# Reordering the first batch of a linear-attention and SwiGLU kernel: k's exp and maximum earlier, the second q.z between two k.v terms

## The chip, the cores and the metric

One core of one Trainium2 chip. The metric is device time in microseconds (us) of the whole kernel, one number per run, compared as medians. Ratios are the mean time of one kernel's fast runs over the mean of the other's fast runs of the same rounds, so they are not quite the ratio of the medians quoted beside them. Times within a profile are us from the span's start. In its lines PE is TensorE, PEld TensorE's loading of weights, DVE VectorE, ACT ScalarE and POOL GpSimd; L292 is line 292 of the kernel. The granted clock is the share of its full clock that TensorE was given; each run comes with its mean.

## The reference

```python
def phi(x):                                   # elu(x) + 1
    return np.where(x > 0, x, np.exp(x) - 1.0) + 1.0
q_p, k_p = phi(q), phi(k)                     # batch 8, heads 8, seq 576, dim 64
kv  = einsum('bhsd,bhse->bhde', k_p, v)
z   = sum(k_p, axis=2)
x   = (q_p @ kv) / (q_p . z + 1e-6)           # 4608 x 512 after a transpose
out = (silu(x @ w_gate) * (x @ w_val)) @ w_out   # 512 -> 1536 -> 512
```

The kernel computes phi as max(x, 0) + min(exp(x), 1). For k these are two tensors, `kp` (the maximum) and `ek` (exp, then the minimum with 1); their sum is phi(k). A product with phi(k) can be taken as one term of the sum, or as two terms that TensorE accumulates.

## The kernel before

The long middle of the kernel is layer 1 and layer 2 of the feed-forward block (`l1`, the matmuls of L292, and `l2`, L299). Before it stands a prologue for batch 0, scheduled by hand. In its profile each engine's instructions come in the order of these calls: k's first half landed at 7.43, but its maximum, which stands behind three q products on VectorE, ran at 8.56.

```python
    # helpers, cut to their effect (lp: first or second half of the heads)
    # exp_k(b,lp)  ScalarE  ek = exp(k)              mx_k  VectorE  kp = max(k, 0)
    # mn_k         VectorE  ek = min(ek, 1)          add_k VectorE  kp = ek + kp
    # q_exp/q_phi  ScalarE / VectorE: the same for q, transposed, four pieces
    # zt(.., kp|ek)        TensorE  sum over the sequence (z), term by term
    # zr_copy              VectorE  Zr <- PSUM
    # t_corners(g, Zr|R)   TensorE  q.z or q.kv, four 64x64 corners
    # lnrd                 ScalarE  rd = exp(-ln(q.z)), two pieces of 512 columns
    # kv_corner(.., kp|ek) TensorE  k.v, 36 small matmuls;  r_copy VectorE  R <- PSUM
    # x_t                  VectorE  xT = q.kv * rd (one PSUM bank each)
    # l1_mm(g, f, ps, c)   TensorE  chunk c of layer 1 (L276)
    # warm(n)              TensorE  n idle matmuls on ones
    ...
    q_exp(1, 0, qb)
    q_exp(1, 1, qb)
    exp_k(0, 0)
    warm(WARM[2])
    exp_k(0, 1)
    q_phi(0, 0, qa); q_phi(0, 1, qa); q_phi(1, 0, qb)
    mx_k(0, 0)
    q_phi(1, 1, qb)
    mn_k(0, 0)
    mx_k(0, 1)
    zt(0, 0, X[1], kp, True, False)
    warm(WARM[3])
    zt(0, 0, X[1], ek, False, True)
    zr_copy(0, 0, X[1])
    warm(WARM[4])
    t_corners(0, Zr, 0, pp4[2])
    lnrd(pp4[2], 0)
    add_k(0, 0)
    mn_k(0, 1)
    zt(0, 1, Y[0], kp, True, False)
    kv_corner(0, 0, kp, True, True)
    r_copy(0, 0, 1, "VV")
    zt(0, 1, Y[0], ek, False, True)
    warm(WARM[5], ps=X[0])
    zr_copy(0, 1, Y[0])
    t_corners(0, R, 0, X)
    x_t(0, 0, X, (0,))
    kv_corner(0, 1, kp, True, False)
    kv_corner(0, 1, ek, False, True)
    r_copy(0, 1, 2, "VV")
    t_corners(0, Zr, 1, Y)
    lnrd(Y, 1)
    x_t(0, 0, X, (1,))
    l1_mm(0, 0, pp4[2], (0,))
    l1_mm(0, 1, X, (0,))        # its second bank is the one that x_t(.., (1,)) reads
    t_corners(0, R, 1, pp4[1])
    x_t(0, 1, pp4[1])
    for c in (1, 2, 3):
        l1_mm(0, 0, pp4[2], (c,)); l1_mm(0, 1, X, (c,))
    ...
```

## Time and profile before

| | before |
|---|---|
| median of the first runs | 313.73 us (313.45 to 314.19) |
| span of the profiled run | 311.8 us |
| TensorE busy | 98% of the span |
| TensorE's share of the chain that ended last | 95% |
| first matmul of L292, layer 1 at full width | 18.18 us |
| third q exp on ScalarE (a reference point used below) | 7.23 us |

In the profile a matmul of L292 lasts 0.38 us and the next one starts 0.22 us after it: the records overlap, so TensorE's busy share is not what to aim at. What the reader needs is where TensorE waits, and after 18.18 us it practically doesn't. The prediction below shows the chain and VectorE's timeline. ScalarE's timeline of the kernel before (columns: start, length, engine, line, operation, written and read tile, shape, count).

```profile
6.41 2.09 ACT L120 ACTIVATE qT<-pp,m 128x512 f16<-128x512 f32 x3
8.39 2.21 ACT L120 ACTIVATE ek<-kr 128x1152 f16<-128x1152 f16 x2
```

k's two exps start at 8.39, right behind q's last piece, and no idle time is noted before them: they wait for ScalarE, not for the load of k, which landed at 7.43.

### The profile page before, as it was taken

The numbers are of one execution on the slowest core, as the hardware profiler recorded it, in microseconds if no ns is written. First come the engines' busy times: TensorE is split into PE (matmuls) and PEld (weight loads), VectorE is DVE, ScalarE is ACT, GpSimd is POOL, SyncE is SP. The second block draws the span as 40 slices with busy tenths as digits, with TensorE's granted clock in tenths as the row PEclk, the third lists the DMA queues.
The fourth block names the chain that finished last, engine by engine and source line by source line (L and its number), as shares of the span: only waits on it lengthen the run. The fifth ranks groups of instructions, "written<-read, shape, count | busy, mean of one in ns | idle before, by whom it ended". The sixth has DMA issues, their size and how long they took to land.

```text
span 311.8 us, 5565 instructions
## 1 busy us (share of the span) xinstructions
PE 305.4 (98%) x2206; PEld 142.0 (46%) x2206; DVE 205.1 (66%) x361; ACT 152.7 (49%) x231; POOL 48.7 (16%) x73
## 2 busy tenths in 40 slices
PE   7999999999999999999999999999999999999994
PEld 3444454444544454445444544454444444444442
DVE  4855878999599658976697759874981434143410
ACT  4865959538733844374536643574330333033311
POOL 8745444400000410041000500000000000000000
PEclk9999999999999999999999999999999999999998
DMA  8999999999502593239512990323032300240014
GB/s 216 196 198 200 206 206 236 235 206 148 116 15 39 98 196 109 40 58 189 156 38 41 132 233 13 63 52 87 0 75 60 78 1 1 45 92 0 2 34 101
DMA packets 41178, 32.80 MB, mean 105 GB/s; under 512 B 16448, under 2 KB 36160, under 8 KB 41152
## 3 DMA queue, kind: packets, MB, share of 16 engines
q0 software_dynamic: 20480, 18.29, 37.4%
q1 hardware_dynamic: 20592, 14.13, 19.1%
q8 instruction: 17, 0.28, 0.3%
q14 instruction: 9, 0.07, 0.1%
q10 hardware_dynamic: 80, 0.03, 0.0%
HBM read 37.75 MB, written 9.44 MB: 151 GB/s over the span
## 4 chain that ended last, share of the span: by engine, by line
PE 95%; DVE 2%; DMA 1%; SPq 0%; issue 0%; ACT 0%; DVEq 0%
PE pp L292 58%; PE pp L299 30%; PE pp L276 2%; PE pp L254 2%; PE pp L185 2%; DMA q<-in_q_dram 1%; DVE qT L454 1%; PE pp L124 1%; DVE xT L425 0%; PE pp L412 0%; PE pp L212 0%; PE pp L374 0%; DVE osb L322 0%; SPq L333 0%; DVE qp L467 0%
## 5 line engine op out<-in xcount | busy, mean ns | idle before, releaser
L120 ACT ACTIVATE sil<-pp 128x512 f16<-128x512 f32 x108 | 63.4, 597 | 100.8 <-PE pp L292 98.4
L292 PE MATMUL pp<-xT,wg 128*128 128x512 f16 x416 | 106.8, 379 | 0.0
L292 PE MATMUL pp<-xT,wv 128*128 128x512 f16 x416 | 106.8, 379 | 0.0
L285 DVE SCALAR_TENSOR_TENSOR hT<-pp,sil 128x512 f16<-128x512 f32 x108 | 72.3, 681 | 48.0 <-PE pp L292 35.3
L299 PE MATMUL pp<-wo,hT 128*128 128x512 f16 (+2 forms) x444 | 97.1, 373 | 0.6 <-DVE osb L322 0.6
L299 PEld LDWEIGHTS <-hT 128*128 128x128 f16 x444 | 41.9, 98 | 49.9 <-issue 2.1
L292 PEld LDWEIGHTS <-wv 128*128 128x128 f16 x416 | 40.7, 98 | 49.1
L292 PEld LDWEIGHTS <-wg 128*128 128x128 f16 x416 | 40.7, 98 | 48.5
L322 DVE TENSOR_SCALAR osb<-pp 128x512 f32<-128x512 f32 (+1 forms) x19 | 12.9, 681 | 31.1 <-PE pp L299 26.7
L120 ACT ACTIVATE osb<-pp 128x512 f32<-128x512 f32 (+1 forms) x18 | 10.3, 574 | 34.8 <-PE pp L299 34.8
L120 ACT ACT_TABLE_LOAD x13 | 16.7, 1283 | 2.5 <-PE pp L292 2.4
L120 ACT ACTIVATE ek<-kr 128x1152 f16<-128x1152 f16 x16 | 17.8, 1157 | 0.1
L710 POOL COPY gate<-qT 128x1 f16<-128x1 f16 x4 | 1.5, 374 | 95.9 <-DMA qT<-qp 95.9
L229 DVE TENSOR_TENSOR qp<-qp,rden 128x1152 f16<-128x1152 f16 x12 | 16.2, 1347 | 0.0
L220 DVE TENSOR_REDUCE den<-prod 128x18 f32<-128x1152 f16 x12 | 16.1, 1342 | 0.0
L120 ACT ACTIVATE eq<-qr 128x1152 f16<-128x1152 f16 x14 | 15.6, 1151 | 0.1
L271 DVE TENSOR_SCALAR xT<-pp 128x512 f16<-128x512 f32 (+1 forms) x14 | 8.8, 667 | 6.8 <-PE pp L254 6.8
L103 POOL DMA_DIRECT2D vr<-in_v_dram x16 | 11.8, 740 | 8.8 <-DMA wo<-in_moe_w_out_dram 2.4
L103 POOL DMA_DIRECT2D kr<-in_k_dram x16 | 11.5, 722 | 7.9 <-DMA wo<-in_moe_w_out_dram 1.9
L159 DVE TENSOR_TENSOR kp<-ek,kp 128x1152 f16<-128x1152 f16 x15 | 11.4, 758 | 0.5
L147 DVE TENSOR_SCALAR ek<-ek 128x1152 f16<-128x1152 f16 x16 | 8.0, 500 | 5.0 <-ACT ek L120 5.0
L103 POOL DMA_DIRECT2D qr<-in_q_dram x14 | 10.1, 724 | 5.6 <-DMA qr<-in_q_dram 2.6
(86 smaller groups left out, 180.0 us busy)
## 6 DMA issues: line engine op xcount, KB each, us to landing
out_dram<-osb SPq DMA_DIRECT2D x70, 128.0 KB, 2.8
kr<-in_k_dram POOLq DMA_DIRECT2D x16, 288.0 KB, 8.7
vr<-in_v_dram POOLq DMA_DIRECT2D x16, 288.0 KB, 9.7
qr<-in_q_dram POOLq DMA_DIRECT2D x14, 288.0 KB, 11.6
wg<-in_moe_w_gate_dram POOLq DMA_DIRECT2D x5, 256.0 KB, 9.5
wv<-in_moe_w_val_dram POOLq DMA_DIRECT2D x5, 256.0 KB, 10.1
q<-in_q_dram SPq DMA_DIRECT2D x2, 576.0 KB, 4.2
wo<-in_moe_w_out_dram POOLq DMA_DIRECT2D x2, 512.0 KB, 12.4
```

The lines of the kernel that those rows point to most:

```text
L103: nc.gpsimd.dma_start(out=dst[b % NB][:, 2 * lp:2 * lp + 2, :], in_=src[b].rearrange("(l a) (c j) d -> (a c) l (j d)", a=2, j=J)[:, 2 * lp ...
L120: nc.scalar.activation(out=out, in_=in_, func=func, bias=bias, scale=scale)
L147: nc.vector.tensor_scalar(out=a, in0=a, scalar1=1.0, scalar2=None, op0=ALU.min)
L159: nc.vector.tensor_tensor(out=a, in0=ek[b % 2][:, lp, :, :], in1=a, op=ALU.add)
L185: nc.tensor.matmul(out=ps[hh][D * l2:D * l2 + D, D * lp:D * lp + D], lhsT=t[b % 2][rows, lp, j, D * l2:D * l2 + D], rhs=vr[b % NB][rows, 2 ...
L220: nc.vector.tensor_reduce(out=den[:, c, :], in_=prod[:, :, :].rearrange("p j (l d) -> p (j l) d", d=D), axis=AX.X, op=ALU.add)
L229: nc.vector.tensor_tensor(out=qv, in0=qv, in1=rden[:, c, :].unsqueeze(2).to_broadcast([P, 2 * J, D]), op=ALU.mult)
L271: nc.vector.tensor_scalar(out=dst, in0=ps[l2][:, c0:], scalar1=1.0 / SC, scalar2=None, op0=ALU.mult)
L285: nc.vector.scalar_tensor_tensor(out=hT[g % 2][:, fb, :], in0=ps[1][:, :], scalar=SC, in1=s[:, :], op0=ALU.mult, op1=ALU.mult)
L292: nc.tensor.matmul(out=ps[h][:, :], lhsT=w[:, c, P * fb:P * fb + P], rhs=xT[g % 2][:, c, :], start=(c == 0), stop=(c == 3))
L299: nc.tensor.matmul(out=l2p[(g, t)][:, n0:n1], lhsT=hT[g % 2][:, fb, P * t:P * t + P], rhs=wo[:, fb, n0:n1], start=(fb == 0), stop=(fb == F ...
L322: nc.vector.tensor_scalar(out=o[:, n0:n1], in0=ps[:, n0:n1], scalar1=1.0 / SC, scalar2=None, op0=ALU.mult)
```

## The change

The intent: start k's first half earlier on ScalarE and VectorE, so that the first z and the first k.v come earlier; take the second half's maximum and minimum out of the way of the first sum; give the second q.z, and with it ScalarE's logarithms, a place ahead of the last k.v term.

```diff
-    WARM = (4, 2, 5, 4, 2, 1)
+    WARM = (4, 2, 5, 2, 2, 1)
     q_exp(1, 0, qb)
+    exp_k(0, 0)
     q_exp(1, 1, qb)
-    exp_k(0, 0)
     ...
+    mx_k(0, 0)
     q_phi(1, 0, qb)
-    mx_k(0, 0)
+    mn_k(0, 0)
     q_phi(1, 1, qb)
-    mn_k(0, 0)
-    mx_k(0, 1)
     ...
     add_k(0, 0)
-    mn_k(0, 1)
-    zt(0, 1, Y[0], kp, True, False)
+    mx_k(0, 1)
     kv_corner(0, 0, kp, True, True)
     r_copy(0, 0, 1, "VV")
-    zt(0, 1, Y[0], ek, False, True)
+    zt(0, 1, Y[0], kp, True, False)
     warm(WARM[5], ps=X[0])
-    zr_copy(0, 1, Y[0])
+    mn_k(0, 1)
     t_corners(0, R, 0, X)
     x_t(0, 0, X, (0,))
+    zt(0, 1, Y[0], ek, False, True)
+    zr_copy(0, 1, Y[0])
     kv_corner(0, 1, kp, True, False)
+    t_corners(0, Zr, 1, Y)
+    lnrd(Y, 1)
     kv_corner(0, 1, ek, False, True)
     r_copy(0, 1, 2, "VV")
-    t_corners(0, Zr, 1, Y)
-    lnrd(Y, 1)
     x_t(0, 0, X, (1,))
```

## The prediction

> **What bounds the kernel now.** I read the page's shares first, then the chain of waits, then the timeline of the first 19 us, because the change touches only the prologue of batch 0.
>
> ```profile
> PE 305.4 (98%) x2206; PEld 142.0 (46%) x2206; DVE 205.1 (66%) x361; ACT 152.7 (49%) x231; POOL 48.7 (16%) x73
> PE 95%; DVE 2%; DMA 1%; SPq 0%; issue 0%; ACT 0%; DVEq 0%
> ```
>
> TensorE carries 95% of the chain that ended last. Listing TensorE's idle gaps from 18.2 us to 306.9 us gives one of 0.03 us and no other over 0.02: once layer 1 runs at full width (L292, from 18.18 us), nothing but TensorE sets the pace. So the change is worth exactly what it does to the start of the first L292 matmul, now 18.18 us. It has no second place to act.
>
> The chain in order of time shows who sets that start:
>
> ```profile
> 8.64 0.38 DVE kp L143
> 9.02 0.05 issue
> 9.07 0.39 PE pp L412 x9
> ...
> 11.11 0.34 PE pp L254 x4
> ...
> 13.19 0.69 DVE xT L425
> 13.88 0.26 DVE R L201 x2
> 14.14 0.66 DVE xT L425
> 14.80 0.04 issue
> 14.85 0.38 PE pp L276
> 15.22 0.34 PE pp L254 x4
> 15.56 2.78 PE pp L276 x12
> 18.34 17.27 PE pp L292 x80
> ```
>
> The chain alternates between VectorE and TensorE until 14.80. The tail is what matters: the second xT product (14.10 to 14.79) frees a PSUM bank; the fourth L276 matmul, which writes that bank, starts at 14.85; behind it on TensorE stand the four last q.kv corners (15.15), then twelve L276 matmuls, then L292. The timeline names the same work:
>
> ```profile
> 9.58 0.62 DVE L147 TENSOR_SCALAR ek<-ek 128x1152 f16<-128x1152 f16 x1
> 10.69 0.29 DVE L416 TENSOR_SCALAR Zr<-pp 128x128 f16<-128x128 f32 x1
> 12.54 0.29 DVE L416 TENSOR_SCALAR Zr<-pp 128x128 f16<-128x128 f32 x1
> 13.19 0.69 DVE L425 SCALAR_TENSOR_TENSOR xT<-pp,rd 128x512 f16<-128x512 f32 x1 [0.36 <-PE pp L254]
> 13.79 0.35 DVE L201 CAST R<-pp 128x64 f16<-128x64 f32 x2
> 14.10 0.69 DVE L425 SCALAR_TENSOR_TENSOR xT<-pp,rd 128x512 f16<-128x512 f32 x1
> 15.67 0.69 DVE L425 SCALAR_TENSOR_TENSOR xT<-pp,rd 128x512 f16<-128x512 f32 x1 [0.87 <-PE pp L254]
> 16.58 0.69 DVE L425 SCALAR_TENSOR_TENSOR xT<-pp,rd 128x512 f16<-128x512 f32 x1 [0.22 <-ACT rd L120]
> ```
>
> Two chains end nearly together. The third product (15.67) releases chunk 2 of layer 1 at 16.41; the fourth waits for ScalarE's last reciprocal (ends 16.54) and releases chunk 3 at 17.32. Both must move for a gain; either alone can cause a loss.
>
> [...] k's first half landed at 7.43 us, yet its maximum (L143) ran only at 8.56, behind the third q product. [...] Here 512-column matmuls start 0.42 us apart at 1.06 us and 0.22 apart from 9.32 on; no idle gap is over 0.6 us[...]. [...] the minimum of ek took 0.62 us at 9.58, inside a GpSimd DMA issue (9.21 to 9.95), and 0.45 at 11.56, in a pause of it; that is 0.17 more, not a wait to the issue's end.
>
> **The change, part by part.** All durations are from this trace. "Pitch" is start to start where nothing waits: a q exp 0.59, a k exp 1.05, a 128x512 product on VectorE 0.61, a Zr copy 0.21, two R copies 0.30 to the next operation.
>
> *Front half: k's exp, maximum and minimum earlier.* The third q exp starts at 7.23; k's first exp follows at 7.82 (was 8.39) and ends at 8.98. The fourth q exp goes from 7.82 to 8.87, ending 9.55; the second k exp stays at 9.44. On VectorE, k's maximum starts at 7.26 + 0.61 = 7.87, the third q product at 8.23, k's minimum at 8.98 + 0.03 = 9.01 instead of 9.58. The fourth q product waits for its exp: 9.55 + 0.03 = 9.58. The Zr copy stands behind it, 9.58 + 0.61 = 10.19, against 10.69 now. Gain 0.50; the hoped-for 0.57 is clipped by the late q exp. Two warm-up matmuls (0.43 us) go out between the two k sums, which needs them gone: the second sum can now start near 9.5.
>
> *Middle.* Moving the second half's maximum and minimum behind the sum changes little on the path, since the sum started right after the Zr copy before as well: 10.19 + 0.21 = 10.40, ending 11.15. First k.v at 11.20 (was 11.70), R copies at 11.20 + 0.53 = 11.73, ready 12.09, R corners at 12.17 (was 12.67), first xT product at 12.17 + 0.52 = 12.69 (was 13.19). Still 0.50 ahead.
>
> *Tail: the new order of the second half.* Here the gain is spent. The second Zr copy was at 12.54, before the first product; now the minimum precedes and the second z sum follows the R corners, so the copy stands behind the first product: 12.69 + 0.61 = 13.30, ready 13.59. [...] the second q.z corners start at 13.59 + 0.06 = 13.65 (were at 13.50), and the second term of the last k.v, placed after them, at 13.65 + 0.24 = 13.89 (was 13.20). The R copies wait for that term, 0.53 after its start as in the first k.v: 14.42 (were 13.79, held there only by the first product). The second xT product is behind the R copies: 14.42 + 0.31 = 14.73, against 14.10. That is +0.63 on the chain shown. From there everything repeats: fourth L276 matmul 15.48 (14.85), last corners 15.79 (15.15), third product 16.30 (15.67), chunk 2 at 17.05 (16.41), then eight matmuls of 0.215: L292 at 18.77, against 18.18.
>
> *ScalarE's side.* Its second group of logarithms starts 0.45 after the corners, 14.10 against 13.98, so its last reciprocal ends at about 16.66 instead of 16.54. The fourth product would then run at 16.91, before chunk 3 needs it at 17.91. This chain no longer decides.
>
> Sum: −0.50 at the first product, +1.09 between first and second product (2.04 from start to start, was 0.91, less rounding), −0.05 where chunk 3 no longer waits: about **+0.6 us**. 313.73 + 0.59 = **314.3 us**. None of the removed or moved work was itself 2% of anything: 2% is 6.3 us, a third of the prologue.
>
> **The rivals.**
> 1. *The front gain survives.* If the author's intent holds, that is, if the second q.z corners start early and ScalarE's chain is the true bound, everything shifts by 0.4 to 0.5: 313.3. For it: the chain of waits runs through the first Zr copy, which does move. Against it: VectorE's order puts the R copies ahead of the second product in the changed kernel too, and they now wait for a k.v term that itself waits for the second Zr copy. This round trip was absent before.
> 2. *Only ScalarE's delay counts.* If I have the R copies too late, the logarithms' later start gives +0.1: 313.85.
> 3. *The clock relapses.* Two warm-up matmuls fewer, and new TensorE gaps of 0.3 us near 9.3 and 0.65 near 14.8. [...] Against it: before, TensorE already idled 0.56 us at 9.07, and was busy again.
> 4. *A load becomes the bound.* k's exp and maximum now want k at 7.8; it landed at 7.43, 0.4 to spare. The loads of v (10.40, 11.79) are needed at 11.20 and 12.8. A load later by 0.5 would undo the front gain, which adds at most 0.3 to the end.
>
> **Range and chances.** The three unprofiled times of before span 0.74 us, so a median may be off by 0.3; my steps of 0.02 to 0.06 add up to perhaps 0.25. That gives 313.8 to 314.8; for rivals 1, 2 and 3 I widen it to 313.6 to 315.0. Two per cent in either direction is out of reach of the stretch touched: faster 0.005, slower 0.01, the rest within.
>
> **What would show it.** Right: first Zr copy near 10.2; first xT product near 12.7; second Zr copy after it, near 13.3; the two last R copies near 14.4 with a wait for k.v (L185) before them; second xT product near 14.7; the fourth L276 matmul with about 0.65 us of TensorE idle before it; first L292 near 18.8. Wrong: R copies that start at 13.8 or sooner, or a first L292 before 18.2; matmuls of L276 0.43 apart would mean the clock; an exp of k with a wait for its load would mean rival 4.

Passages that no trace or run of this case bears out are cut from it, and the cuts are marked. The sum is −0.50, +1.09 and −0.05, put as about +0.6 us, and the forecast 313.73 + 0.59 = 314.3 us. That fewer warm-up matmuls and new gaps might lower the clock was the author's guess: the trace of the kernel before has a granted clock of 1.00 from 6.8 to 306.9 us. The tail's step from the q.z corners to the second k.v term took for granted that TensorE keeps the order of its calls; the changed kernel's trace shows that order (under "Why the prediction was right or wrong").

## The result

Changed 314.48 us (median of 4 runs, 314.39 to 314.52), before 313.59 us (4 runs, 313.40 to 314.19). The ratio is 1.0025, 95% interval 1.0007 to 1.0042: slower by a quarter of a per cent, which is "same" by the 2% measure. Both profiled runs are at a mean granted clock of 0.997.

The page of the changed kernel: busy shares, then the chain's shares by engine.

```profile
PE 305.6 (98%) x2204; PEld 141.9 (45%) x2204; DVE 204.5 (65%) x361; ACT 152.7 (49%) x231; POOL 48.6 (16%) x73
PE 95%; DVE 2%; DMA 2%; ACT 1%; issue 0%; SPq 0%; DVEq 0%
```

Nothing here tells the two kernels apart: four TensorE instructions fewer (two warm-up matmuls and their weight loads), the same shares. The chain in order of time does (start, length, what):

```profile
8.22 1.06 ACT ek L120
9.28 0.59 ACT qT L120
9.86 0.02 issue
9.89 0.69 DVE qT L454
10.58 0.20 DVE Zr L416
10.78 0.68 DVE kp L159
...
12.98 0.69 DVE xT L425
13.67 0.21 DVE Zr L416
13.88 0.04 issue
13.92 0.41 PE pp L254 x4
14.33 0.41 PE pp L185 x36
14.74 0.35 DVE R L201 x2
15.09 0.61 DVE xT L425
15.70 0.04 issue
15.74 0.38 PE pp L276
```

The chain runs from the first xT product (12.98) to the second Zr copy, the q.z corners, the k.v term, the R copies and the second product (15.09), where the chain of before went straight from the first product to the R copies and the second product. VectorE's timeline of the changed kernel shows the same and what it waited for (in brackets: idle time, and who ended it):

```profile
10.50 0.28 DVE L416 TENSOR_SCALAR Zr<-pp 128x128 f16<-128x128 f32 x1
12.98 0.69 DVE L425 SCALAR_TENSOR_TENSOR xT<-pp,rd 128x512 f16<-128x512 f32 x1 [0.23 <-PE pp L254]
13.59 0.28 DVE L416 TENSOR_SCALAR Zr<-pp 128x128 f16<-128x128 f32 x1
14.73 0.36 DVE L201 CAST R<-pp 128x64 f16<-128x64 f32 x2 [0.86 <-PE pp L185]
15.00 0.68 DVE L425 SCALAR_TENSOR_TENSOR xT<-pp,rd 128x512 f16<-128x512 f32 x1
```

VectorE stands idle for 0.86 us before the R copies, for k.v (L185). The first full L292 matmul starts at 19.03, 0.85 after that of before, and after it TensorE has one gap over 0.02 us up to the last batch, as before. The prologue's loss arrives whole at the end: in all 14 profiles of this document, 293.5 to 293.7 us pass from the first L292 matmul to the end of the span.

Part of the 0.85 has nothing to do with the order. The third q exp, which the change does not touch, started at 7.53 in this profile instead of 7.23, because q's second half landed at 6.07 instead of 5.90 and its cast then took 0.62 us instead of 0.43. So I compare the kernels by the **distance** from the third q exp to the first L292 matmul: 10.95 before, 11.50 changed, +0.55. The prediction's own times give 18.77 − 7.23 = 11.54.

### The profile page after: what moved, and what is told of

Read it like the earlier page. It is cut to its first block, busy times and chain, and to the rows that moved or that the text cites. A ratio compares the mean times of both kernels' runs of the same rounds, so it can differ in the third digit from the quotient of the medians.

```text
span 312.6 us, 5561 instructions
## 1 busy us (share of the span) xinstructions
PE 305.6 (98%) x2204; PEld 141.9 (45%) x2204; DVE 204.5 (65%) x361; ACT 152.7 (49%) x231; POOL 48.6 (16%) x73
## 4 chain that ended last, share of the span: by engine, by line
PE 95%; DVE 2%; DMA 2%; ACT 1%; issue 0%; SPq 0%; DVEq 0%
PE pp L292 57%; PE pp L299 30%; PE pp L276 2%; PE pp L254 2%; PE pp L185 2%; DMA q<-in_q_dram 2%; DVE xT L425 0%; ACT qT L120 0%; ACT ek L120 0%; DVE qT L454 0%; DVE kp L159 0%; PE pp L212 0%; DVE qp L467 0%; PE pp L374 0%; DVE osb L322 0%
## 5 line engine op out<-in xcount | busy, mean ns | idle before, releaser
L292 PE MATMUL pp<-xT,wg 128*128 128x512 f16 x416 | 106.8, 379 | 0.0
L292 PE MATMUL pp<-xT,wv 128*128 128x512 f16 x416 | 106.8, 379 | 0.0
L292 PEld LDWEIGHTS <-wv 128*128 128x128 f16 x416 | 40.7, 98 | 49.1
L292 PEld LDWEIGHTS <-wg 128*128 128x128 f16 x416 | 40.7, 98 | 48.4
```

The lines of the kernel that those rows point to most:

```text
L292: nc.tensor.matmul(out=ps[h][:, :], lhsT=w[:, c, P * fb:P * fb + P], rhs=xT[g % 2][:, c, :], start=(c == 0), stop=(c == 3))
```

## The experiments

Each was run in 5 rounds beside the kernel before and gave the reference's result. "k exp" is the start of the first k exp, "k lands" the landing of the half that it reads.

| run | median us | before beside it | ratio (95% interval) | distance | k lands | k exp |
|---|---|---|---|---|---|---|
| again | 314.34 | 313.53 | 1.0025 (1.0012 to 1.0037) | 11.72 | 8.00 | 8.03 |
| front_old_tail | 313.27 | 313.53 | 0.9989 (0.9975 to 1.0002) | 11.22 | 8.35 | 8.37 |
| new_tail_only | 314.51 | 313.53 | 1.0030 (1.0018 to 1.0043) | 11.91 | 7.35 | 8.35 |
| qz_behind | 313.91 | 313.53 | 1.0011 (0.9999 to 1.0024) | 11.11 | 7.48 | 8.16 |
| warm_four | 314.19 | 313.46 | 1.0023 (1.0011 to 1.0035) | 12.01 | 8.30 | 8.32 |
| x_before_r | 314.02 | 313.46 | 1.0027 (1.0010 to 1.0043) | 11.32 | 7.64 | 7.81 |
| before_k_swapped | 314.51 | 313.46 | 1.0032 (1.0016 to 1.0049) | 11.60 | 9.20 | 9.22 |
| changed_k_swapped | 316.27 | 313.46 | 1.0083 (1.0059 to 1.0107) | 14.04 | 8.89 | 8.91 |
| front_again | 313.84 | 313.55 | 1.0017 (0.9994 to 1.0041) | 10.51 | 7.25 | 7.81 |
| front_k_first | 313.34 | 313.55 | 0.9992 (0.9979 to 1.0004) | 10.51 | 7.43 | 7.98 |
| x_warm_four | 313.73 | 313.55 | 1.0005 (0.9993 to 1.0017) | 11.05 | 7.20 | 7.82 |
| front_k_first_warm | 313.61 | 313.69 | 0.9999 (0.9985 to 1.0012) | 10.70 | 7.68 | 7.98 |

Distance, landing and exp are of one profiled run each; the medians are of five or six runs, of which the profiled one need not be typical. The record numbers four different chips for the four sets of rounds, so absolute times are compared only within a set, as in the column "before beside it".

### The changed kernel again

No edit.

> The changed kernel once more, for a closer ratio and a second profile. In the one profile so far the third q exp started at 7.53 us, against 7.23 before, because q's second half landed later; from there to the first full layer 1 matmul (L292) it took 11.50 us, against 10.95 before. Theory A (the order of the tail costs it): that distance is a property of the order and comes back at 11.50 within 0.1, whatever the start of the third q exp, and the kernel is 0.5 to 0.7 us over the one before (ratio 1.0016 to 1.0022). Theory B (the later landing was part of the cost, for a reason in the change): the third q exp starts near 7.5 again and the kernel is 0.8 to 0.9 us over.

The third q exp was back at 7.22 and the kernel still 0.81 us over: theory B fell. But the distance was 11.72, not 11.50, so theory A was not the whole either. The difference, 0.22, is just what the first k exp lost: it started 0.81 after the third q exp instead of 0.59, because k's load landed at 8.00. A theory F came from this: by calling for k at 7.82 instead of 8.39, the change put the load of k on the path.

### The front with the old tail

```diff
 # from the changed kernel
-    mx_k(0, 1)
-    kv_corner(0, 0, ..); r_copy(0, 0, 1, ..); zt(0, 1, .., kp, ..); warm(..)
-    mn_k(0, 1); t_corners(0, R, 0, X); x_t(0, 0, X, (0,))
-    zt(0, 1, .., ek, ..); zr_copy(0, 1, ..)
-    kv_corner(0, 1, kp, ..); t_corners(0, Zr, 1, Y); lnrd(Y, 1)
-    kv_corner(0, 1, ek, ..); r_copy(0, 1, 2, ..)
+    mx_k(0, 1); mn_k(0, 1)
+    kv_corner(0, 0, ..); r_copy(0, 0, 1, ..)
+    zt(0, 1, .., kp, ..); zt(0, 1, .., ek, ..); zr_copy(0, 1, ..)
+    t_corners(0, R, 0, X); x_t(0, 0, X, (0,))
+    kv_corner(0, 1, kp, ..); kv_corner(0, 1, ek, ..); r_copy(0, 1, 2, ..)
+    t_corners(0, Zr, 1, Y); lnrd(Y, 1)
```

The warm-up matmul of the tail (`WARM[5]`) is dropped as well.

> The changed front (k's first exp, maximum, minimum early; second maximum and minimum behind the sum), with the second z sum, its Zr copy and both terms of the last k.v in the order of the kernel before. Theory A (the gain of the front is real and the tail ate it): first xT product 0.4 to 0.5 us earlier than before counted from the third q exp, second product about 0.42 earlier, first L292 10.5 us after the third q exp (10.95 before); 0.3 to 0.5 us faster than the kernel before. Theory C (ScalarE's chain or a load takes over, so the front gives nothing): within 0.1 us of the kernel before.

Four of its five runs were at 313.05 to 313.28, about 0.3 under the kernel before; the fifth, the profiled one, at 313.96. ScalarE's timeline of that run shows the larger part of why:

```profile
8.37 1.16 ACT L120 ACTIVATE ek<-kr 128x1152 f16<-128x1152 f16 x1 [0.40 <-DMA kr<-in_k_dram]
```

The exp waited 0.40 us for the load of k, a wait that the kernel before could not have had at that time, as its exp starts at 8.39 anyway. (Its second-half minimum also took 0.65 us instead of 0.45.) The interval does not exclude 1. The same kernel was run again:

> The front of the changed kernel with the tail of the one before, once more, to settle whether it beats the kernel before (0.9989, interval 0.9975 to 1.0002; its one profile had k's load at 8.35 us, 0.9 late, and was its slowest run). Theory A with theory F: 0.3 us faster in most runs, no gain or a small loss [...]; median ratio 0.9988 to 0.9993. If the gain of the front is not real: 1.000 within 0.0005.

In its profile k landed at 7.25, and the working of the prediction is met nearly to the digit: first Zr copy 10.18 (10.19 predicted), first xT product 12.77 (12.69 predicted), and with the old tail a distance of 10.51, 0.44 less than before. VectorE's timeline of it:

```profile
10.18 0.28 DVE L416 TENSOR_SCALAR Zr<-pp 128x128 f16<-128x128 f32 x1
12.77 0.69 DVE L425 SCALAR_TENSOR_TENSOR xT<-pp,rd 128x512 f16<-128x512 f32 x1
13.37 0.35 DVE L201 CAST R<-pp 128x64 f16<-128x64 f32 x2
13.63 0.68 DVE L425 SCALAR_TENSOR_TENSOR xT<-pp,rd 128x512 f16<-128x512 f32 x1
```

That profiled run took 313.23; of the five others four took 313.77 to 314.25, and one 316.18. So the median missed the expectation, while the mechanism in the profile did not: the gain of the front exists in a run whose load is on time, and it is not reliable. What the others waited for is not known, as only one run of each kernel is profiled. The run of 316.18 differs in one recorded number: its granted clock was 0.986, that of the five others 0.997 to 1.000.

### The old front with the new tail

```diff
 # from the kernel before; its front, and from the first k.v on:
-    mn_k(0, 1); zt(0, 1, .., kp, ..)
     kv_corner(0, 0, ..); r_copy(0, 0, 1, ..)
-    zt(0, 1, .., ek, ..); warm(..); zr_copy(0, 1, ..)
+    zt(0, 1, .., kp, ..); warm(..); mn_k(0, 1)
     t_corners(0, R, 0, X); x_t(0, 0, X, (0,))
+    zt(0, 1, .., ek, ..); zr_copy(0, 1, ..)
     kv_corner(0, 1, kp, ..)
+    t_corners(0, Zr, 1, Y); lnrd(Y, 1)
     kv_corner(0, 1, ek, ..); r_copy(0, 1, 2, ..)
-    t_corners(0, Zr, 1, Y); lnrd(Y, 1)
```

> The front of the kernel before with the changed tail alone. Theory A: first xT product where it was (5.96 us after the third q exp), the R copies wait for the second term of k.v, second product 1.1 us later than before, first L292 12.0 us after the third q exp; 1.0 to 1.2 us slower than the kernel before. Theory D (the front, its two missing warm-up matmuls or its order, makes the loss, and the tail is harmless): within 0.2 us of the kernel before.

Slower by 0.98 us, distance 11.91 (12.0 expected): the tail alone makes a loss larger than the whole change. VectorE's timeline:

```profile
13.06 0.69 DVE L425 SCALAR_TENSOR_TENSOR xT<-pp,rd 128x512 f16<-128x512 f32 x1
13.67 0.28 DVE L416 TENSOR_SCALAR Zr<-pp 128x128 f16<-128x128 f32 x1
14.81 0.36 DVE L201 CAST R<-pp 128x64 f16<-128x64 f32 x2 [0.86 <-PE pp L185]
15.09 0.68 DVE L425 SCALAR_TENSOR_TENSOR xT<-pp,rd 128x512 f16<-128x512 f32 x1
```

The same 0.86 us of idleness before the R copies as in the changed kernel. The distance of the changed kernel is 0.41 less (11.50): what the front gives back. Theory D (the front does the harm) fell.

### The second q.z behind both k.v terms

```diff
 # from the changed kernel
     kv_corner(0, 1, kp, True, False)
-    t_corners(0, Zr, 1, Y)
-    lnrd(Y, 1)
     kv_corner(0, 1, ek, False, True)
     r_copy(0, 1, 2, "VV")
+    t_corners(0, Zr, 1, Y)
+    lnrd(Y, 1)
```

> The changed kernel with one thing undone: the second q.z corners (and their logarithms) behind both terms of the last k.v, not between them. Theory A: the R copies no longer wait for the second Zr copy; second xT product at about 6.7 us after the third q exp (6.87 before, 7.47 changed); then ScalarE's last reciprocal decides, first L292 at 11.07 after the third q exp; 0.1 us slower than the kernel before, 0.45 faster than the changed one. Theory E (the late second Zr copy alone is the cost, wherever the corners stand): no faster than the changed kernel.

313.91 against the changed kernel's 314.34 in the same rounds: 0.43 of the loss hangs on this one place. The distance is 11.11 (11.07 expected), though the second product came 6.97 after the third q exp, not 6.7. In VectorE's timeline the wait for k.v is shorter, and the last product now waits for ScalarE's reciprocal:

```profile
13.63 0.28 DVE L416 TENSOR_SCALAR Zr<-pp 128x128 f16<-128x128 f32 x1
14.27 0.36 DVE L201 CAST R<-pp 128x64 f16<-128x64 f32 x2 [0.36 <-PE pp L185]
14.54 0.68 DVE L425 SCALAR_TENSOR_TENSOR xT<-pp,rd 128x512 f16<-128x512 f32 x1
...
17.08 0.69 DVE L425 SCALAR_TENSOR_TENSOR xT<-pp,rd 128x512 f16<-128x512 f32 x1 [0.29 <-ACT rd L120]
```

Its Zr copy is as late as in the changed kernel (13.63 and 13.59), so theory E (the late copy alone is the cost) fell. In absolute time it was 0.38 over before where 0.1 was expected; its third q exp was late in the profile (7.57, after a cast of 0.67 us).

### The second product ahead of the R copies

```diff
 # from the changed kernel
     kv_corner(0, 1, ek, False, True)
-    r_copy(0, 1, 2, "VV")
     x_t(0, 0, X, (1,))
+    r_copy(0, 1, 2, "VV")
```

> The changed kernel with the second xT product put ahead of the last two R copies on VectorE, all else as changed. Theory A (the product stands behind R copies that wait for the k.v term behind the second q.z): second product 6.4 us after the third q exp if k's load is on time (7.47 changed), last q.kv corners then wait for the R copies, ScalarE's last reciprocal decides, first L292 at 11.1 after the third q exp; 0.4 to 0.5 us faster than the changed kernel. Theory E (the late Zr copy itself, or ScalarE, is the bound): no more than 0.1 faster than the changed kernel.

Four of six runs at 313.69 to 314.05, two at 315.17 and 315.44. In the profile (a run of 313.99) the second product came 6.51 after the third q exp (7.47 changed), so the queue place was its cost; the distance was 11.32, not 11.1, for a reason not foreseen, the second half's maximum, which took 0.75 us instead of 0.45:

```profile
11.05 0.75 DVE L143 TENSOR_SCALAR kp<-kr 128x1152 f16<-128x1152 f16 x1
```

A DMA issue on GpSimd ran from 10.79 to 11.53, over most of it. That the issue made it longer is not shown: in the kernel before a maximum from 36.18 to 36.63, wholly inside an issue from 36.13 to 36.85, took 0.45. The two slow runs led to another experiment, the same kernel with the warm-up restored:

> x_before_r (four runs at 313.7 to 314.1, two at 315.2 and 315.4, the fast ones profiled at full clock) with the two removed warm-up matmuls back. Theory H (TensorE's clock fell to half [...] in the two slow runs, as the profile of changed_k_swapped shows it from 11.6 to 18.4 us): with more warm-up no run is over 314.6; median 313.9 to 314.1. If the slow runs have another cause: again one or two of five over 315.

No run over 314.15, median 313.73; the maximum took 0.45 in its profile and the distance was 11.05. Five runs without a slow one, against two of six, agree with theory H but do not prove it. The granted clock of each run says more. It was 0.995 in the two slow runs of x_before_r and 0.999 or 1.000 in its four others; in x_warm_four no run was under 0.998. In the profile of changed_k_swapped, below, 6.8 us at half clock go with a granted clock of 0.989 (6.8 × 0.5 / 314.9 is 0.011); by the same arithmetic 0.005 would be some 3 us at half clock (0.005 × 314 / 0.5), an estimate. The only other drop in the profiles comes after the last matmul (in the kernel before from 310.17 to the end, at 0.50) and takes off 0.003 at most. So a drop in the two slow runs is likely; where in the run it lay is not shown.

x_warm_four and warm_four differ only in the place of the second product, and were 0.18 and 0.73 us over the kernel before beside them: 0.55 for that one place.

### The warm-up restored in the changed kernel

```diff
-    WARM = (4, 2, 5, 2, 2, 1)
+    WARM = (4, 2, 5, 4, 2, 1)
```

> The changed kernel with the two removed warm-up matmuls back between the two k sums. Theory A (the tail's order): they fit in TensorE's wait for k's minimum, so nothing moves by more than 0.1 us; 0.6 to 0.9 us over the kernel before, as the changed kernel. Theory G (the missing warm-up costs clock): it is 0.3 us or more faster than the changed kernel.

0.73 us over before (the changed kernel was 0.81 over in other rounds): the missing matmuls are not the loss, and theory G fell. Its profile is again one with k late (8.30): the exp started 1.09 after the third q exp instead of 0.59, and the distance is 12.01 instead of 11.50. An exp 0.50 later made the distance 0.51 longer: the lateness passes through whole.

### A dose of lateness for the load of k

```diff
-    ld2(k, kr, 0)
+    ld(k, kr, 0, 1)
+    ld(k, kr, 0, 0)
```

> A dose of load lateness: the kernel before with the two halves of k's first load issued in the other order, so that the half used first lands second, at about 8.9 us instead of 7.4. Theory F (the kernel before has about 0.9 us of slack on k's first half, which its exp wants at 8.39, and the changed one about 0.4): its exp moves from 8.39 to 8.95, its minimum from 9.58 to 10.14; 0.4 to 0.55 us slower than the kernel before. Without theory F (loads are not on the path in either): no change.

> The same dose in the changed kernel. Theory F: its first k exp moves from 7.82 (load on time) to 8.95, and with it everything on the path, so 1.1 us slower than the changed kernel with its load on time, some 0.9 to 1.1 over its measured median, that is 1.7 to 1.9 us over the kernel before: twice what the same dose costs the kernel before. Without theory F: as the changed kernel, 0.8 over before, or the same surcharge as in the kernel before (0.4 to 0.55).

The kernel before lost 1.05 us by the medians, more than expected, with a wide spread (313.83 to 315.79); in the profile its distance grew by 0.65, the exp by 0.83. The changed kernel lost some 2.0 us more than it had already lost (316.27 − 313.46 − 0.81), again with a wide spread (315.08 to 317.39). That looks like twice the price, as theory F has it, but the medians mix runs of different clocks. Three of the six runs of changed_k_swapped have a granted clock of 0.989 and took 316.64 to 317.39; the three at 0.997 to 1.000 took 315.08, 315.19 and 315.91. The middle one of these is 1.73 over the kernel before, within the 1.7 to 1.9 expected, which is 0.92 more than the changed kernel's own loss. In the kernel before, the five runs at 0.997 or more have a median of 314.22, a loss of 0.76 where 0.4 to 0.55 was expected (its slowest run, 315.79, was at 0.995). So at full clock the dose cost 0.92 and 0.76, which with so few runs is no clear difference; the slower runs are those of the lower clock. The profiled run, of 316.64, is one of those at 0.989. The stretches of the changed kernel with the dose (us, sum, busy time and count of PE, PEld, DVE, ACT, POOL, then granted clock, DMA share and GB/s):

```profile
9.00:11.60 2.60, 1.69 (x22) 0.71 (x22) 2.35 (x6) 2.60 (x3) 1.48 (x2) 1.00 1.25 202
11.60:15.00 3.40, 3.35 (x91) 1.89 (x95) 2.46 (x6) 2.63 (x5) 2.96 (x4) 0.50 1.45 194
15.00:18.40 3.40, 3.30 (x72) 1.48 (x62) 1.30 (x5) 2.26 (x4) 1.61 (x3) 0.50 1.45 197
18.40:21.00 2.60, 2.60 (x15) 1.09 (x14) 1.29 (x2) 1.69 (x3) 1.66 (x3) 1.00 1.45 196
```

From 11.6 to 18.4 us the granted clock was 0.50. TensorE's timeline in it has L276 matmuls 0.42 apart, where 0.22 is usual:

```profile
16.86 0.63 PE L276 MATMUL pp<-xT,wv 128*128 128x512 f16 x1
17.28 0.63 PE L276 MATMUL pp<-xT,wg 128*128 128x512 f16 x1
17.71 0.63 PE L276 MATMUL pp<-xT,wv 128*128 128x512 f16 x1
```

So with the dose came what the prediction's third rival named, a lower clock, in one run by the profile and in two more by their granted clock. What brings it about is not shown. From 8.2 us to the drop at 11.6 TensorE was busy 2.03 us; in the same stretch it was busy 2.67 us in the changed kernel without the dose and 2.83 us in the kernel before, and in neither of these did the clock drop. In the profiles of before_k_swapped and x_before_r it was busy 2.26 and 2.08 us from 9 to 12 us, and the clock stayed at 1.00 from 6 to 24 us as well. What is clean of the clock is the first Zr copy, before the drop: at 11.30, some 1.11 later than the 10.19 of an on-time run (x_warm_four), as expected from the exp (8.91 against 7.82).

### k's first load ahead of the iota, and a search for a better kernel

```diff
 # from front_old_tail
+    ld(k, kr, 0, 0)
     nc.gpsimd.iota(...)
-    ld2(k, kr, 0)
+    ld(k, kr, 0, 1)
```

> The same kernel with k's first half issued ahead of the iota on GpSimd, so some 0.3 to 0.5 us earlier in issue. Theory F (k's landing limits the front): the landing moves to 7.1 to 7.4 us on average, late ones included less often on the path; 0.3 to 0.45 us faster than the kernel before with less spread than front_again. If the queue of the DMA engines, not the issue, sets the landing: same landings as front_again and the same time within 0.1 us.

It landed at 7.43, no sooner than in the kernel before (7.43). But the edit hardly did what it was meant to: in the profile GpSimd started the issue at 1.25 instead of 1.34, only 0.09 us sooner, so whether the issue sets the landing was not tested. All five runs were at 313.27 to 313.50, median 0.21 below the kernel before, whose interval with it still includes 1. With the two warm-up matmuls restored:

> front_k_first (five runs at 313.27 to 313.50, the kernel before 313.55 beside it) with the two removed warm-up matmuls back, as the candidate that beats both kernels. Theory A: no step of the path waits for the warm-up, so first L292 10.5 us after the third q exp again and 313.2 to 313.4 us, 0.2 to 0.3 faster than the kernel before, every run under 313.9. If the two extra matmuls hold up the second k sum: 0.1 to 0.2 us slower than front_k_first.

No gain: 313.61 against 313.69. In its profile the maximum of the second half took 0.65 us (0.45 in front_k_first) and pushed the path by 0.19, the whole difference of the two distances. So there are kernels that beat the changed one; none was shown to beat the kernel before.

## Why the prediction was right or wrong

- **Where it acts.** Right. TensorE has no new gap after the first L292 matmul, and its 0.85 us in the profile is the kernel's 0.89 by the medians within the spread.
- **Front, −0.50.** Right for a run with its loads on time: the first Zr copy is at 10.18 and 10.19 in front_again and x_warm_four, and the old tail turns that into 0.44 less distance. In the changed kernel's profile all of it is shifted by the late third q exp, so that the copy is at 10.50.
- **Tail, second Zr copy behind the first product, then q.z, then k.v, then R copies, then the second product.** Right, and shown piece by piece: from the first product to the second it took 2.02 us in the changed kernel (2.04 predicted, 0.91 before); alone the new tail costs 0.98; with the q.z moved back it costs 0.43 less; with the product ahead of the R copies the product itself is 0.96 sooner counted from the third q exp (6.51 against 7.47). The order of VectorE's queue, on which the prediction rested, is seen here as 0.86 us of idleness before the R copies, with a product behind them whose PSUM bank and reciprocal (13.87 in the changed kernel) were ready; that of TensorE's as a second k.v term whose minimum had ended at 12.75 but which started at 14.16, behind q.z corners that had waited 0.33 us for the Zr copy and started at 13.92. One named sign was weaker than predicted: TensorE idled 0.31 us before the fourth L276 matmul, not 0.65 (0.10 before), although that matmul came when predicted, 0.74 us after the second product's start (0.75 predicted).
- **ScalarE's chain no longer decides.** Right: the fourth product followed the third without a wait in the changed kernel, and in qz_behind, where the second product is earlier, ScalarE decides again (0.29 us of wait).
- **Size, +0.59.** The measured loss is 0.2 to 0.3 larger (0.89 and 0.81 by medians) and inside the range. By the interval of the second set's ratio it is 0.4 to 1.2 us, so the excess is not clear of noise. The distance, 11.50, is within 0.04 of the predicted one. The prediction's written sum has a slip: 2.04 less 0.91 is 1.13, not 1.09, and its terms as written give 0.54; the 0.59 comes from its times (18.77 less 18.18), and these hold.
- **Loads, rival 4.** Mis-sized. The prediction held the load of k to have 0.4 us to spare and to cost at most 0.3. In the 12 profiled runs in which k's halves were loaded in the usual order, the first half landed between 7.20 and 8.35, in four of them at 8.00 or later. (All four call for k early, but only two of the 12 do not, so this shows no link.) In two profiles of the changed tail (again, warm_four) the lateness appears in full, 0.22 and 0.50, in the distance. In the first profile of the changed kernel k came at 8.09, just in time for an exp at 8.12; there the extra 0.30 is q's late load and cast. That such lateness makes up the rest of the medians is an inference; only single runs are profiled.
- **Clock, rival 3.** It did not act in the changed kernel (granted clock 1.00 from 6.8 to 21 us, and restoring the warm-up gained nothing clear of the spread), but it was nearer than I thought: with k's exp 1.09 us later (8.91 against 7.82) it came in three runs of six, in one by the profile and in the two others by their granted clock, also 0.989.

What stays open: the slow runs of x_before_r and front_again (315.2 to 316.2). Their granted clocks, 0.995, 0.995 and 0.986, are the lowest of their kernels, which speaks for a clock drop as in changed_k_swapped, but none of those runs was the profiled one, so when it fell and whether it makes up all of their time is not shown. Also open is why k lands late in some runs: in the changed kernel's trace 15 of the load's 16 completions had come by 7.50 and the last came at 8.09, 0.59 us behind; in the kernel before it came 0.14 us behind the fifteenth, at 7.43.

## What to carry to other kernels

When work is moved in an engine's queue, look at what stands behind it as well as at what it waits for: here a copy went behind a product, a matmul group behind that copy, and a product behind that group, so a gain of 0.5 us at the start became a loss at the end. A wait that a kernel does not show may still be near: calling for a load 0.6 us sooner (7.82 against 8.39) used up slack that covered the last of its 16 completions (8.09 in the changed kernel's first profile). Compare such small changes from a point that the change does not touch, as 0.3 us of a profile's difference came from before that point.
